# Gated mix of a linear-attention and a softmax-attention block: feature sums on TensorE, denominators in sets of four tiles, projections in four column tiles, placement constants changed

## The chip, the cores and the metric

The kernel runs on one core of one Trainium2 chip. The metric is the device time of one execution in microseconds (us). Before the change it is 698.01 us, the median of three runs (697.92 to 698.1). A measurement of this kernel can tell about 0.2% from no change.

## The reference

Input x has 2048 rows of 512. Two blocks with their own weights read it, each with 32 heads of 16, and a sigmoid gate mixes their outputs row by row.

```python
g = sigmoid((x * gate_w).sum(-1, keepdims=True))
# A, linear attention
q, k, v = heads(x @ A_wqkv)
pq = einsum("bhsd,hdf->bhsf", q, w_phi);  pk = the same of k
phi_q = concat([softmax(pq), softmax(-pq)]);  phi_k = the same of pk
kv = einsum("bhsf,bhsd->bhfd", phi_k, v);  z = phi_k.sum over s
a = merge((phi_q @ kv) / (phi_q @ z + 1e-6)) @ A_wo
# B, softmax attention
b = merge(softmax(q k^T / 4) v) @ B_wo
return g * a + (1 - g) * b
```

Each softmax of A goes over 16 features; its sum is called a feature sum below. There are 64 of them for a row of x: 8 groups of heads (g), plus and minus (s), 4 heads (j). With the exponentials left undivided, the query side needs only the ratio of the plus sum to the minus sum, and the plus sum times 1e-6 in the denominator.

## The kernel before, in words

Softmax attention is most of the work: 2048 score tiles of 128 keys by 512 queries, 64 for each of 32 blocks. A block (b) is one chunk of 512 queries and four heads, which lie in four row strips of 32 on TensorE. A score tile takes one of two ways:

- ScalarE: a pair of tiles goes into two PSUM banks (`add_qk`, L874, product at L870) and one ACTIVATE of 128x1024 makes exponentials (`add_exp`, L961). The two pairs of banks alternate, and the results go to a ring of twelve buffers (E). These pairs, 683 of them, are the slots j = 0 to 682.
- VectorE: the table DN (L31) says how many tiles of each block go there, 682 in all. A tile goes into one of three spare banks (named MISC in the code); VectorE turns it into the bits of an approximate exponential (L947, or two tiles at once, L937); GpSimd adds constants to groups of up to four such tiles (`shifted`, L923), so that three terms with shifted errors are summed.

The products with the values (L982) write psO: four heads lie side by side in four column strips of 32, so that four matmuls make one round. At a block's end VectorE copies psO (L1076), and a chain of small DMAs and VectorE steps divides by the sums.

Everything else runs in the gaps, through the same three spare banks: projections of x and the output projections (`proj`, L664, matmul at L665, full 128x128 weights), the features of the linear branch (`phi`, L1228) and their sums (L1245, one reduce of 1024 elements for each tile of 128 rows), kv and z (`kv_half`, L1275), and on the query side `q_rest` (L1326): for each of 16 row tiles two fills with numerators and denominators together, then for each fill a sum (L1338), a reciprocal (L1341) and a scaling (L1347). `fill` (L635) puts matmuls into a bank, `drain` (L657) is what empties it.

The order on each engine is fixed when the program is built. `Plan.layout` (L178) walks through time with a duration, a priority and dependencies for each operation, picks the next one of each engine, and hands out the banks. Score pairs have the first priority (-100), products with the values -50, further terms T_PRIO, and the rest runs by due times made of constants at L31 to L74 (K_AT and K_PACE for the key side, Q_AT and Q_PACE for the query side, O_AT for outputs, SHIFT for the VectorE tiles of each block). Where TensorE would have nothing to do, and a measure of its recent activity is under ACTIVE[0], the plan puts in a round of four matmuls with zeros (L972). `PE_CLASS` (L45) names three shapes of operation on TensorE: row strips, column strips, and the rest; a change of shape is given 0.105 us in the plan. On the chip each engine then runs its list in order and waits on semaphores.

Of the kernel before, what the change touches and what calls it, by code (L numbers as in the profile page):

```python
# [9 lines left out]
F32 = mybir.dt.float32  # L10
# [20 lines left out]
DN = (6, 20, 18, 20, 26, 22, 22, 20, 22, 18, 20, 18, 22, 20, 22, 22, 26, 22, 22, 28, 22, 24, 22, 26, 18, 22, 26, 18, 20, 20, 28, 20)  # L31
# [4 lines left out]
STICK = 13.196  # L36
UNITS = 564.8
W_AT = 24.588
D_FIRST = 26
# [7 lines left out]
DQ_PRIO, DQ_K = 0.569, 1.599  # L47
KG_AT, KG_PACE, QG_AT, QG_PACE = 21.949, 5.386, 233.655, 11.179
R1_AT, R1_PACE, R2_AT, R2_PACE, R3_AT, R3_PACE = 34.139, 13.567, 134.03, 16.806, 277.767, 5.95
TR_LAT, TR_ISSUE = 3.0, 0.4  # L50
OP_AT, OP_PACE = 603.737, 4.0
SPLIT = (14, 15)
O_AT, O_PACE = 500.39, 18.839
# [3 lines left out]
QK_TOL = (0.374, 0.198)  # L57
TURN_PAD = -0.09
# [3 lines left out]
SHIFT = (-13.58, 13.8, -12.95, 1.31, -8.83, -3.06, 3.59, -1.48, -3.29, 1.96, -3.19, 0.72, 14.4, 6.88, 13.75, 4.89, 8.7, 7.61, 0.14, -2.86, -5.22, -8.15, -0.83, -3.77, 7.8, 2.53, -1.02, -12.66, -5.29, -0.23, -14.57, -12.4)  # L62
P64, W64 = 0.19, 0.21
M_LATE = -26.949
QK_PAD = 0.02
D1_PAIR = 1.13
PAIR_WAIT = 0.05
D_AHEAD = 21.848
CONT = -56.63
# [50 lines left out]
class Plan:  # L120
# [57 lines left out]
    def layout(self):  # L178
# [21 lines left out]
        while left:  # L200
# [30 lines left out]
            for e in ENGINES:  # L231
# [11 lines left out]
                if e == "pe" and last_pe not in (None, "zero") and busy[e] > t - 1e-6:  # L243
# [233 lines left out]
def _build(ctx, nc, A_x, A_wqkv, A_w_phi, A_wo, B_wqkv, B_wo, gate_w, out):  # L477
# [32 lines left out]
    statq = sb([128, 8, 64], F32, name="statq")  # L510
# [16 lines left out]
    denr = sb([128, 2, 32], F32, name="denr")  # L527
# [106 lines left out]

    def fill(prio, mms, reads, banks=None, name="", chunk=1, dur=MM, after=(), cols=NQ, cont=CONT):  # L635

        f = Fill(MISC if banks is None else banks)
        prev = None
        for i in range(0, len(mms), chunk):
# [9 lines left out]
            op.full, op.fill = cols / 2400.0 * len(part), True  # L649
# [14 lines left out]
    def proj(lhs, rhs):  # L664
        return [lambda e, ap, i=i: e.matmul(ap, lhsT=lhs[i], rhs=rhs[i], start=(i == 0), stop=(i == len(lhs) - 1))  # L665
                for i in range(len(lhs))]
# [26 lines left out]
    def k_fill(r, c, prio, banks=None, eng="dve"):  # L693
        f, mm = fill(prio, proj([W_B[:, t, D + 128 * r:D + 128 * (r + 1)] for t in range(KT)],
                                [xT[:, t, NQ * c:NQ * (c + 1)] for t in range(KT)]), ["wbk" if r else "wbk0"] + xk(c), banks,
                     name=f"K{r}.{c}")
# [71 lines left out]
    def q_fill(m, prio, banks=None, after=()):  # L768
# [3 lines left out]
                     name=f"Q{r}.{qc}", after=after)  # L772
# [367 lines left out]
    def last_mm(tile):  # L1140
        return [lambda e, ap: e.matmul(ap, lhsT=oT[:, 3, tile // 4, 128 * (tile % 4):128 * (tile % 4) + 128],
                                       rhs=WoB[:, 3, :], start=True, stop=True)]

    def out_tile(qc, i):
        tile = 4 * qc + i
        if tile in SPLIT:
            f, mm = fill(O_AT + O_PACE * tile, last_mm(tile), [("oT", qc, 3), "WoB"], name=f"O{tile}")
# [5 lines left out]
        f, mm = fill(O_AT + O_PACE * (4 * qc + i), mms, reads, name=f"O{tile}")  # L1153
# [8 lines left out]
    def out_part(n):  # L1162
        tile = SPLIT[n]
        mms, reads = out_mms(tile, range(3), True)
        f, mm = fill(OP_AT + OP_PACE * n, mms, reads, name=f"OP{tile}")
# [5 lines left out]
    def out_last(i):  # L1171
        tile = 12 + i
        mms, reads = out_mms(tile, range(KT), True)
        if i < 2:
            f, mm = fill(-45, mms[:7], reads[:-2] + reads[-1:], banks=MISC + bS[:lowS], name=f"O{tile}", after=last_d1 + o_mms, cont=-45)
            last = P.add("pe", 0.25, -200 + i, lambda e: mms[7](e, f.ap()), reads=[("oT", 3, 3)], after=[mm],
                         name=f"O{tile}.7")
            last.full = 0.215
# [3 lines left out]
        else:  # L1182
            f, mm = fill(-200 + i - 1.5, last_mm(tile), [("oT", 3, 3), "WoB"], banks=bS[:lowS], name=f"O{tile}")
# [30 lines left out]
    def va_fill(st, prio, after):  # L1214
        m, b = st % 8, st % 2
        f, mm = fill(prio, proj([xT[:, t, 128 * st:128 * (st + 1)] for t in range(KT)],
                                [WvA[:, t, :] for t in range(KT)]), ["WvA"] + xk(st // 4), name=f"VA{st}", after=after)
        va_ops.append(mm)
        by = stat[:, b, :].rearrange("p (g s j) -> p g s j", s=2, j=4)
        for s in range(2):  # L1220
# [3 lines left out]
                reads=[("rs", b), ("ss", b)], writes=[("vA", m, s)], name=f"VAe{st}.{s}", last=s == 1)  # L1224
        P.add("pool", 0.3, prio, lambda e: e.tensor_copy(vA[:, m, :, :, 64:68], by), reads=[("rs", b), ("ss", b)],
              writes=[("vA", m, 2)], name=f"VAr{st}")

    def phi(qk, st, prio):  # L1228
# [4 lines left out]
                     xk(st // 4) + [("Wp", qk, t) for t in range(KT)], name=f"P{qk}.{st}",  # L1233
# [3 lines left out]
        def both(e, ap):  # L1237
            for sgn in range(2):
# [4 lines left out]
        e3 = dst.rearrange("p (g f) -> p g f", f=DH)  # L1243
        sums, skey = (stat[:, b, :], ("ss", b)) if qk else (statq[:, st % 8, :], ("sq", st % 8))
        P.add("dve", 1.22, prio, lambda e: e.tensor_reduce(sums, e3, AX.X, ALU.add), reads=[dkey], writes=[skey],  # L1245
              name=f"ss{qk}.{st}")
        if b == 0:
            return
        if qk == 0:
            both_q = statq[:, st % 8 - 1:st % 8 + 1, :].rearrange("p b (g s j) -> p (b g) s j", s=2, j=4)  # L1250
            r3 = ratio[:].rearrange("p b (g j) -> p (b g) j", j=4)
            P.add("dve", 0.4, prio, lambda e: e.reciprocal(r3, both_q[:, :, 1, :]), reads=[("sq", st % 8 - 1), ("sq", st % 8)],
                  writes=["ratio"], name=f"rs{qk}.{st}")
            P.add("dve", 0.25, prio, lambda e: e.tensor_tensor(r3, r3, both_q[:, :, 0, :], ALU.mult),
                  reads=["ratio", ("sq", st % 8 - 1), ("sq", st % 8)], writes=["ratio"], name=f"rt{qk}.{st}").lock = True
            for i in (st - 1, st):
                scaled_q(i, prio)
            return
        P.add("dve", 0.62, prio, lambda e: e.reciprocal(stat[:], stat[:]), reads=[("ss", 0), ("ss", 1)],
              writes=[("rs", 0), ("rs", 1)], name=f"rs{qk}.{st}")  # L1260
        for i in (st - 1, st):
            va_fill(i, prio, [P.ops[-2]] if i == st - 1 else ())
# [148 lines left out]
    for n in range(4):  # L1411
# [3 lines left out]
        for i in range(4 * n, 4 * n + 4):  # L1415
            q_rest(i, Q_AT - 1.0 + Q_PACE * (i + 4))
# [84 lines left out]
```

## Time and profile before

| | |
|---|---|
| median of the runs shown | 698.01 us |
| profiled execution, its own time | 699.61 us |
| its span, first to last instruction | 697.6 us |
| TensorE busy (PE) | 676.3 us, 97% |
| ScalarE busy (ACT) | 671.3 us, 96% |
| VectorE busy (DVE) | 606.4 us, 87% |
| GpSimd busy (POOL) | 369.8 us, 53% |
| exponentials, L961 | 683, 641.6 us |
| feature sums, L1245 | 32, 38.5 us |
| granted TensorE clock | 1.0 throughout |

In the rows of the profile a group of instructions is given by line, engine, operation, output and inputs, shape and count, then its busy time in us and the mean of one in ns, then how long the engine stood idle just before them and what released it. Busy times count overlapping instructions once, so a mean times its count can be more than the busy time. In the timeline the columns are start and length in us, then the group; a line can hold several merged instructions (x3). A line's shape 128*32 is a matmul with 128 rows and 32 columns of weights, 32*128 one with 32 rows and 128 columns. A busy TensorE is not TensorE at its peak, since matmuls are pipelined.

### The profile page before, as it was taken

To read this page: it belongs to the slowest core of one execution; us is meant where nothing else is said; L and a number is where in the kernel's file an instruction comes from. 1 tells how busy PE (TensorE), PEld (TensorE's weight loads), DVE (VectorE), ACT (ScalarE), POOL (GpSimd) and SP (SyncE) were. 2 spreads that over 40 slices of the span, in tenths; PEclk is the share of its full clock that TensorE was granted. 3 is DMA by queue.
4 is the path that set the end of the run, shared out by engine and by line. 5 is a ranking of instruction groups with operands and counts; after the bars stand their busy time and mean duration, and the time that the engine had idled before them with its cause. 6 is when DMAs were issued, how large, how long until landed. Compare 5 with 4: busy or idle time off the path is not lost.

```text
span 697.6 us, 17633 instructions
## 1 busy us (share of the span) xinstructions
PE 676.3 (97%) x7281; PEld 217.7 (31%) x7335; DVE 606.4 (87%) x1020; ACT 671.3 (96%) x754; POOL 369.8 (53%) x407
## 2 busy tenths in 40 slices
PE   9999999999999999999999999999999999999999
PEld 4332233323323223333322322332223322232323
DVE  4689679998988798999987999999999998988882
ACT  6999999999999999999999999999999999999995
POOL 7165246474556552453555674657657555455542
PEclk9999999999999999999999999999999999999999
DMA  6700001001000100100003012223311123314221
GB/s 130 173 12 17 20 18 24 10 11 24 9 18 11 25 10 5 22 10 11 19 11 97 26 27 80 52 49 58 86 51 38 50 46 87 86 48 115 64 58 50
DMA packets 67455, 30.74 MB, mean 44 GB/s; under 512 B 52696, under 2 KB 62296, under 8 KB 67376
## 3 DMA queue, kind: packets, MB, share of 16 engines
q1 hardware_dynamic: 66368, 28.95, 17.7%
q8 instruction: 57, 0.93, 0.6%
q10 hardware_dynamic: 576, 0.52, 0.2%
q0 software_dynamic: 432, 0.15, 0.1%
q14 instruction: 22, 0.18, 0.1%
HBM read 7.87 MB, written 8.88 MB: 24 GB/s over the span
## 4 chain that ended last, share of the span: by engine, by line
PE 63%; DVE 18%; ACT 16%; issue 2%; DMA 1%; SPq 0%; DVEq 0%
PE psO L982 23%; PE psS L870 22%; ACT E_t L961 15%; PE psS L665 11%; PE psO L972 4%; DVE Tx_t L947 3%; DVE Ty_t L947 3%; DVE Wp_t L947 2%; DVE vA_t L947 1%; DVE oT_t L947 1%; ACT phiK_t L1239 1%; DVE stat_t L1245 1%; DVE Tz_t L947 1%; PE psS L735 1%; DMA ld<-Tf_t 1%
## 5 line engine op out<-in xcount | busy, mean ns | idle before, releaser
L961 ACT ACTIVATE E_t<-psS 128x1024 bf16<-128x1024 f32 x683 | 641.6, 1059 | 12.2 <-PE psS L870 5.8
L870 PE MATMUL psS<-qz_t,kTB_t 32*128 32x512 bf16 x2048 | 279.8, 385 | 13.8 <-ACT E_t L961 5.0
L947 DVE TENSOR_SCALAR Tx_t<-psS 128x512 int16<-128x512 f32 x218 | 144.3, 682 | 15.8 <-PE psS L870 15.0
L870 PEld LDWEIGHTS psS<-qz_t,kTB_t 32*128 32x128 bf16 x2048 | 73.4, 91 | 248.4 <-ACT E_t L961 194.1
L982 PE MATMUL psO<-E_t,vaug_t 128*32 128x512 bf16 (+1 forms) x1366 | 112.8, 385 | 0.3 <-issue 0.3
L923 POOL INT64_ADD vA_t<-vA_t x67 | 66.2, 993 | 33.8 <-PE psO L982 23.9
L947 DVE TENSOR_SCALAR Ty_t<-psS 128x512 int16<-128x512 f32 x112 | 74.0, 680 | 7.3 <-PE psS L870 7.0
L923 POOL INT64_ADD Ty_t<-Tx_t x27 | 27.2, 1006 | 64.1 <-DVE Tx_t L947 55.5
L972 PE MATMUL psO<-xT_t,zero_t 128*32 128x512 bf16 x648 | 57.4, 386 | 0.8 <-DVE Tf_t L1076 0.5
L923 POOL INT64_ADD Ty_t<-Ty_t x38 | 38.2, 1004 | 15.8 <-PE psO L982 12.7
L982 PE MATMUL psO<-vA_t,vaug_t 128*32 128x512 bf16 (+1 forms) x480 | 46.1, 383 | 0.0
L947 DVE TENSOR_SCALAR WAT_t<-psS 128x512 int16<-128x512 f32 x58 | 38.2, 679 | 3.6 <-PE psS L870 3.4
L982 PE MATMUL psO<-Ty_t,vaug_t 128*32 128x512 bf16 x398 | 40.5, 384 | 0.0
L947 DVE TENSOR_SCALAR oT_t<-psS 128x512 int16<-128x512 f32 x56 | 37.3, 684 | 3.6 <-PE psS L870 3.6
L947 DVE TENSOR_SCALAR Wp_t<-psS 128x512 int16<-128x512 f32 x58 | 38.9, 682 | 1.2 <-PE psS L870 1.1
L947 DVE TENSOR_SCALAR Tz_t<-psS 128x512 int16<-128x512 f32 x54 | 36.1, 682 | 3.5 <-PE psS L870 3.3
L947 DVE TENSOR_SCALAR vA_t<-psS 128x512 int16<-128x512 f32 x56 | 36.8, 681 | 1.0 <-PE psS L870 0.6
L982 PEld LDWEIGHTS psO<-E_t,vaug_t 128*32 128x32 bf16 x1366 | 24.3, 95 | 41.9 <-issue 39.1
L665 PE MATMUL psS<-Wp_t,xT_t 128*128 128x512 bf16 x116 | 35.6, 384 | 0.9 <-issue 0.5
L665 PE MATMUL psS<-xT_t,WB_t 128*128 128x512 bf16 x96 | 29.7, 385 | 0.8 <-issue 0.6
L923 POOL INT64_ADD vA_t<-Tx_t x20 | 18.2, 910 | 20.6 <-DVE Tx_t L947 17.3
L923 POOL INT64_ADD WoB_t<-oT_t x17 | 16.8, 987 | 21.6 <-DVE oT_t L947 21.3
(160 smaller groups left out, 870.8 us busy)
## 6 DMA issues: line engine op xcount, KB each, us to landing
dpq<-EA_t SPq DMA_DIRECT2D x16, 256.0 KB, 2.1
Rb_t<-lr SPq DMA_DIRECT2D x120, 32.0 KB, 1.8
dpo<-kv_t SPq DMA_DIRECT2D x16, 128.0 KB, 1.8
qz_t<-qz_t SPq DMA_DIRECT2D x120, 16.0 KB, 1.8
Tf_t<-Tf_t SPq DMA_DIRECT2D x60, 32.0 KB, 2.0
WB_t<-in_B_wqkv_dram SPq DMA_DIRECT2D x3, 384.0 KB, 4.4
out_dram<-WvA_t SPq DMA_DIRECT2D x8, 128.0 KB, 1.9
out_dram<-WB_t SPq DMA_DIRECT2D x6, 128.0 KB, 1.8
```

The lines of the kernel that those rows point to most:

```text
L665: return [lambda e, ap, i=i: e.matmul(ap, lhsT=lhs[i], rhs=rhs[i], start=(i == 0), stop=(i == len(lhs) - 1)) for i in range(len(lhs))]
L735: mms = [lambda e, ap, i=i, t=t: e.matmul(ap[:, 256 * i:256 * (i + 1)], lhsT=xT[:, t, NQ * c + 128 * (2 * hf + i):NQ * c + 128 * (2 * hf + ...
L870: return e.matmul(bank, lhsT=kT_B[32 * i:32 * i + 32, ROW[b // 2] % 2, 128 * kt:128 * (kt + 1)], rhs=qz[32 * i:32 * i + 32, b // 2 % 4, b ...
L923: op = P.add("pool", P64 + W64 * size, d_prio(g["ts"][0]) - 5.0 + (0.0 if key == "s" else M_LATE), lambda e: e.int64_add(words(dst), words ...
L947: ops.append(drain(f, mm, "dve", 0.70, d_prio(d), lambda e, ap, q=q: e.tensor_scalar(quarter(tb, q).bitcast(I16), ap, EXPB, 0.0, op0=ALU.a ...
L961: op = P.add("act", 0.051 + 0.4267 * n, 0.0, lambda e: e.activation(Ebuf[:, j // 2 % EPAIRS, 512 * SZ[0] * (j % 2):512 * SZ[0] * (j % 2) + ...
L972: ins = e.matmul((psO if bank is None else bank)[32 * i:32 * i + 32, :], lhsT=zero[:], rhs=xT[:, 0, 0:NQ], start=bank is not None, stop=ba ...
L982: return e.matmul(psO[32 * i:32 * i + w, :], lhsT=vaug[:, kt, o:o + w], rhs=rhs, start=start, stop=stop, tile_position=(0, 32 * i), skip_g ...
L1239: ins = e.activation(dst.rearrange("p (g s c) -> p s g c", s=2, c=64)[:, sgn, :, :], ap.rearrange("p (g c) -> p g c", c=64), ACTF.Exp, sca ...
L1245: P.add("dve", 1.22, prio, lambda e: e.tensor_reduce(sums, e3, AX.X, ALU.add), reads=[dkey], writes=[skey], name=f"ss{qk}.{st}")
```

## The change

1. The feature sums move from VectorE to TensorE. For two row tiles together, 16 matmuls with an identity as weights add up the 16 features of each head in PSUM; matmul n reads every 16th element, from n on, of both tiles, 128 columns. VectorE then takes reciprocals straight from PSUM (and, on the query side, copies the plus sums).
2. The denominators of the linear branch are made for four row tiles at once (`z_rest`: 32 matmuls of 4 columns, one sum, one reciprocal), and the numerators of a row tile in one fill of eight matmuls with one scaling of 128x512.
3. Each projection matmul (128x128 weights, 512 columns) becomes four matmuls of 32 weight columns in the four column strips, and has the shape of the products with the values in the plan (`"col"`, class 1).
4. The constants of the plan are other ones, among them DN (sum 682 before, 686 after).

```diff
-DN = (6, 20, 18, 20, 26, 22, 22, 20, 22, 18, 20, 18, 22, 20, 22, 22, 26, 22, 22, 28, 22, 24, 22, 26, 18, 22, 26, 18, 20, 20, 28, 20)
+DN = (6, 20, 18, 20, 26, 26, 22, 20, 22, 18, 20, 18, 16, 18, 22, 22, 26, 22, 20, 28, 20, 24, 22, 26, 18, 22, 26, 18, 22, 24, 28, 26)
...
-STICK = 13.196
+STICK = -4.158
...
-ACTIVE = (1.3, 0.464, 0.202, 0.534)
-PE_CLASS = {"qk": 0, "dq": 0, "pv": 1, "term": 1, "zero": 1}
-T_PRIO = 24.777
+ACTIVE = (1.766, 0.586, 0.369, 0.433)
+PE_CLASS = {"qk": 0, "dq": 0, "pv": 1, "term": 1, "zero": 1, "col": 1}
+T_PRIO = 63.423
...
-OP_AT, OP_PACE = 603.737, 4.0
+OP_AT, OP_PACE = 662.103, 4.0
...
-O_AT, O_PACE = 500.39, 18.839
+O_AT, O_PACE = 464.624, 20.512
...
-G_DEEP = 9
-K_AT, K_PACE, Q_AT, Q_PACE = 75.929, 11.329, 287.016, 9.116
+G_DEEP = 13
+K_AT, K_PACE, Q_AT, Q_PACE = 75.929, 11.329, 323.294, 8.77
...
+    def columns(e, out, lhsT, rhs, start, stop):
+        for i in range(4):
+            ins = e.matmul(out[32 * i:32 * i + 32, :], lhsT=lhsT[:, 32 * i:32 * i + 32], rhs=rhs, start=start, stop=stop,
+                           tile_position=(0, 32 * i))
+        return ins
...
     def proj(lhs, rhs):
-        return [lambda e, ap, i=i: e.matmul(ap, lhsT=lhs[i], rhs=rhs[i], start=(i == 0), stop=(i == len(lhs) - 1))
+        return [lambda e, ap, i=i: columns(e, ap, lhs[i], rhs[i], i == 0, i == len(lhs) - 1)
                 for i in range(len(lhs))]
...
-        e3 = dst.rearrange("p (g f) -> p g f", f=DH)
-        sums, skey = (stat[:, b, :], ("ss", b)) if qk else (statq[:, st % 8, :], ("sq", st % 8))
-        P.add("dve", 1.22, prio, lambda e: e.tensor_reduce(sums, e3, AX.X, ALU.add), reads=[dkey], writes=[skey],
-              name=f"ss{qk}.{st}")
         if b == 0:
             return
+        m = st % 8 - 1 if qk else 0
+        pair = (phiK if qk else EA)[:, m:m + 2, :].rearrange("p b (g f) -> p b g f", f=DH)
+        mms = [lambda e, ap, n=n: e.matmul(ap[:, 0:128].rearrange("p (b g) -> p b g", b=2), lhsT=ident[:], rhs=pair[:, :, :, n],
+                                           start=(n == 0), stop=(n == DH - 1)) for n in range(DH)]
+        f, mm = fill(prio, mms, ["ident"] + [("phiK" if qk else "EA", m), ("phiK" if qk else "EA", m + 1)], name=f"S{qk}.{st}",
+                     chunk=4, dur=0.057, cols=128)
...
-        P.add("dve", 0.62, prio, lambda e: e.reciprocal(stat[:], stat[:]), reads=[("ss", 0), ("ss", 1)],
-              writes=[("rs", 0), ("rs", 1)], name=f"rs{qk}.{st}")
+        drain(f, mm, "dve", 0.9, prio, lambda e, ap: e.reciprocal(flat(stat[:]), ap[:, 0:128]), writes=[("rs", 0), ("rs", 1)],
+              name=f"rs{qk}.{st}")
...
+    def z_rest(n, prio):
+        mms = [lambda e, ap, j=j, g=g: e.matmul(ap[:, 32 * j + 4 * g:32 * j + 4 * g + 4], lhsT=qT(g)[:, 128 * j:128 * (j + 1)],
+                                                rhs=kzbd[:, g, 64:68], start=True, stop=True) for j in range(4) for g in range(8)]
+        f, mm = fill(prio, mms, [("phiQT", g) for g in range(8)] + ["kz1"], name=f"Z{n}", chunk=8, dur=0.028, cols=60, after=n_ops[-1:])
+        n_ops.append(mm)
+        dr = denr[:, n % 2, :]
+        plus = flat(statq[:, 4 * (n % 2):4 * (n % 2) + 4, :])
+        drain(f, mm, "dve", 0.25, -3, lambda e, ap: e.scalar_tensor_tensor(dr, plus, 1e-6, ap[:, 0:128], ALU.mult, ALU.add),
+              reads=[("sq", 4 * (n % 2) + j) for j in range(4)], writes=[("dr", n % 2)], name=f"na{n}")
+        P.add("dve", 0.9, -3, lambda e: e.reciprocal(dr, dr), reads=[("dr", n % 2)], writes=[("dr", n % 2)], name=f"nb{n}")
```

The lines left out pass the name "col" to the fills of projections, shape the numerators into one fill, and give other values to the remaining constants (SHIFT for all blocks, the due times of the value and key projections, and pads of a few hundredths).

More of the change, by code (lines that the diff above doesn't have):

```diff
@@ L242, in layout @@
                     active = sum(w * (y - max(x, t - WINDOW)) for x, y, w in streams) / WINDOW
-                if e == "pe" and last_pe not in (None, "zero") and busy[e] > t - 1e-6:
+                if e == "pe" and last_pe not in (None, "zero", "col") and busy[e] > t - 1e-6:
                     want = {"qk": "dq", "dq": "dq"}.get(last_pe, "term")
@@ L648, in fill @@
                        after=after if prev is None else [prev], name=f"{name}.{i}")
-            op.full, op.fill = cols / 2400.0 * len(part), True
+            op.full, op.fill, op.kind = cols / 2400.0 * len(part), True, kind
             if prev is None:
@@ L1182, in out_last @@
         else:
-            f, mm = fill(-200 + i - 1.5, last_mm(tile), [("oT", 3, 3), "WoB"], banks=bS[:lowS], name=f"O{tile}")
+            f, mm = fill(-200 + i - 1.5, last_mm(tile), [("oT", 3, 3), "WoB"], banks=bS[:lowS], name=f"O{tile}", kind="col")
             with_part(tile, f, mm)
@@ L1216, in va_fill @@
         f, mm = fill(prio, proj([xT[:, t, 128 * st:128 * (st + 1)] for t in range(KT)],
-                                [WvA[:, t, :] for t in range(KT)]), ["WvA"] + xk(st // 4), name=f"VA{st}", after=after)
+                                [WvA[:, t, :] for t in range(KT)]), ["WvA"] + xk(st // 4), name=f"VA{st}", after=after, kind="col")
         va_ops.append(mm)
```

102 lines of the change are left out of this document (46 added, 56 removed).

## The prediction

> **What bounds the kernel now.** I read the page's first part, then the groups by shape, the chain that ended last, and the timeline of ScalarE, of the stretch from 300 to 312 us and of the end.
>
> ```profile
> PE 676.3 (97%) x7281; PEld 217.7 (31%) x7335; DVE 606.4 (87%) x1020; ACT 671.3 (96%) x754; POOL 369.8 (53%) x407
> ...
> L961 ACT ACTIVATE E_t<-psS 128x1024 bf16<-128x1024 f32 x683 | 641.6, 1059 | 12.2 <-PE psS L870 5.8
> ```
>
> TensorE and ScalarE are both nearly full, but TensorE's 97% holds filler: the rows of L972, products with zeros put where the plan had nothing else, are 57.4 + 5.0 us. It needs 676.3 - 62.4 = 614 us. ScalarE has no filler. What an exponential costs when nothing holds it up is read from unbroken runs in the chain:
>
> ```profile
> 48.77 12.04 ACT E_t L961 x13
> ...
> 168.04 0.99 ACT phiK_t L1239 x2
> ...
> 327.26 17.53 ACT E_t L961 x19
> ```
>
> 12.04 / 13 = 0.926 and 17.53 / 19 = 0.923 us for each; 0.98 us for the two activations of a feature tile (0.99 with the step to the next). So 683 x 0.923 + 32 x 0.98 = 661.8 us of work from 8.7 (start of the first exponential) to 687.6 (end of the last, below). 678.9 us passed, so ScalarE stood or was slowed for 17.1 us. The five longest pauses:
>
> ```profile
> 137.94 2.86 ACT L961 ACTIVATE E_t<-psS 128x1024 bf16<-128x1024 f32 x3 [0.96 <-PE psS L870]
> ...
> 346.25 17.93 ACT L961 ACTIVATE E_t<-psS 128x1024 bf16<-128x1024 f32 x19 [1.47 <-PE psO L982]
> ...
> 376.61 10.33 ACT L961 ACTIVATE E_t<-psS 128x1024 bf16<-128x1024 f32 x11 [1.15 <-PE psS L870]
> 388.15 1.94 ACT L961 ACTIVATE E_t<-psS 128x1024 bf16<-128x1024 f32 x2 [1.21 <-PE psO L982]
> ...
> 450.15 4.89 ACT L961 ACTIVATE E_t<-psS 128x1024 bf16<-128x1024 f32 x5 [1.14 <-PE psO L982]
> ```
>
> They sum to 5.9 us. TensorE is named, but it runs a fixed order and is itself held: ahead of 137.9 a score tile waited 0.21 us for a VectorE eviction, ahead of 376.6 one waited 1.03 us for the paired eviction of L937, which stood behind two reciprocals. Ahead of 388 and 450 TensorE ran filler (four rounds, three rounds) before the last products of a block, which need VectorE's tiles and GpSimd's additions. VectorE was busy 18.8 to 19.9 us of every 20 between 380 and 440. Ahead of 346.3 stands the one 1.45 us mask multiply of L1299. The other 11 us are delays of a few tenths, where a slot holds more TensorE work than 0.92 us.
>
> TensorE's prices, from 300 to 312 us:
>
> ```profile
> 306.98 0.40 PE L982 MATMUL psO<-Ty_t,vaug_t 128*32 128x512 bf16 x4
> ...
> 307.20 0.39 PE L982 MATMUL psO<-oT_t,vaug_t 128*32 128x512 bf16 x4
> 307.53 0.45 PE L870 MATMUL psS<-qz_t,kTB_t 32*128 32x512 bf16 x4
> ```
>
> A round of four 32-column products follows the one before after 0.22 us; the step to score tiles (32*128, rows) takes 0.33. A change of shape costs 0.1 us, into and out of full 128*128 products too (0.32).
>
> And the end:
>
> ```profile
> 679.14 8.44 ACT L961 ACTIVATE E_t<-psS 128x1024 bf16<-128x1024 f32 x9
> ...
> 686.03 0.39 PE L870 MATMUL psS<-qz_t,kTB_t 32*128 32x512 bf16 x2
> ...
> 694.33 2.99 PE L972 MATMUL psS<-xT_t,zero_t 128*32 128x512 bf16 x52
> 694.44 0.69 ACT L1179 ACTIVATE WB_t<-psS,gT_t 128x512 bf16<-128x512 f32 x1 [1.47 <-PE psS L665]
> ```
>
> After the last scores at 686.03 TensorE works without a gap for 8.3 us, until filler starts at 694.33; the last output tile is scaled at 694.44, and its store ends the span 3.2 us later. The end hangs on TensorE, not on ScalarE, which was done at 687.6.
>
> **The change, part by part.** Counts come from the order in which each kernel's instructions stand.
>
> *Exponentials.* Sum of DN 682 -> 686: 1362 score tiles are left to ScalarE, 681 pairs. 2 x 0.923 = **-1.8 us**, on the path.
>
> *VectorE.*
>
> ```profile
> L1245 DVE TENSOR_REDUCE stat_t<-phiK_t 128x64 f32<-128x1024 bf16 x16 | 19.3, 1208 | 3.8 <-ACT phiK_t L1239 3.8
> L1245 DVE TENSOR_REDUCE statq_t<-EA_t 128x64 f32<-128x1024 bf16 x16 | 19.2, 1208 | 3.2 <-ACT EA_t L1239 3.2
> ...
> L722 PE MATMUL psS<-WB_t,xT_t 128*128 128x128 bf16 x128 | 10.6, 221 | 0.2 <-DVE Ty_t L947 0.2
> ...
> L1341 DVE RECIPROCAL denr_t<-denr_t 128x16 f32<-128x16 f32 x32 | 7.2, 239 | 0.3
> ```
>
> Gone: both reduce rows, 38.5; 32 reciprocals, 7.2; 32 sums of L1338, 4.9; 32 scalings of L1347 (128x256), 14.8: 65.4 us. New: 16 scalings of 128x512 from PSUM at 0.745 (the same operation at L1136: 0.746), 11.9; 4 reciprocals of 128x128 at 0.946 (L1259), 3.8; 4 sums of 128x128, between 0.16 (L1338, 16 elements) and 0.48 (256), say 0.3, 1.2; 8 copies of 64, between 0.155 (L1194) and 0.43 (L1292), say 0.2, 1.6. The 16 other reciprocals stay and read PSUM; I know no row for that and add nothing. Evictions of score tiles: 612 -> 606 single at 0.682, 35 -> 40 paired at 1.22: +2.0. Net 65.4 - 20.5 = 45 us less: VectorE 606 -> 561 us (80%). None of this is on the path by itself; it counts by what waits for VectorE.
>
> *TensorE.* Feature sums: 256 products with 128 moving columns. Bounds: 0.056 us each, the spacing of L722 in bursts (contiguous operand), and 0.106, that of the transposes L1356. I take 0.056, the row with the same kind of instruction: +14.3 us (up to 27.1). Denominators by themselves: 128 products of 4 columns at 0.025 (spacing at L1190, one column), +3.2; the numerators stay 128. Two more rounds for the four tiles, +0.4; two score pairs fewer, -0.4. Projections: 440 products become 440 rounds of four, 0.22 either way. Filler: 724 -> 584 products, 35 rounds, -7.7. Changes of shape 1481 -> 1411: -7.0. Sum +2.8 us in the order; without filler +10.5, so it needs 625 us where ScalarE needs 660. What hides the sums is filler and waits for ScalarE; where a stretch has neither, its 0.9 us per pair of tiles delays the next scores. In the trace, TensorE's work between score pairs is over 0.92 us in 245 slots by these prices, in the changed order in 252: I expect the small delays (11 us) to stay as they are.
>
> [...] The sums take every 16th bf16 element, one for each 32 bytes. [...]
>
> *Waits that are added.* The sums wait for both tiles' exponentials and hold one of three spare PSUM banks over some four slots; behind them on TensorE stands everything, score pairs too. The same tiles' reduce waited for the exponentials before (3.8 and 3.2 us idle), without a bank. 16 such fills and 4 for denominators come, 16 numerator fills go. SP's and POOL's instructions are the same but for two additions on POOL (53% busy).
>
> *Pauses.* VectorE with 45 us less, and later with room, should take away the pauses that it and its tiles cause: 0.96, 1.15, 1.21, 1.14, and 0.31 us at 127.8 where two feature tiles meet: **-4.8 us**. The one at 346.3 stays, as the mask multiply does. Bounds: 0 (the order of TensorE is as long, and TensorE is what is late next) and -10 (half the small delays go too).
>
> *The end.* After the last scores the old order has 36 rounds (4 of probabilities, 32 of output projections) in 8.3 us. The new one has 56: one output tile and the rest of another, three sets of probabilities and six more rounds of VectorE's terms stand behind the last scores. 56 x 0.22 + 0.1 = 12.4: **+4.1 us**. It cannot go earlier, since the order is fixed. The last block's chain on VectorE (transpose 0.70, reciprocal 0.25, multiply 0.42, transpose 0.71) ends about 9.3 us after the last scores (30 rounds, then 2.7 as in the trace); its first user stands behind 44 rounds, at 9.8: hidden, by little.
>
> **Sum.** -1.8 - 4.8 + 4.1 = -2.5. The profiled execution took 699.6 (span 697.6 and 2.0 around it) and would be 697.1; it stands 1.6 above the median of 698.0, so the median becomes **695.5 us**.
>
> **Rivals.**
> *A, more goes than the pauses.* Fewer changes of shape (-7.0) fall into slots over 0.92 us, and half of the 11 us of small delays go: 698.0 - 1.8 - 10.3 + 4.1 = 690. For: a projection beside probabilities or terms now costs no change of shape. Against: 252 slots are still over 0.92.
> *B, slower: the work behind the last scores decides.* The pauses stay or are replaced by waits for banks and sums, and the longer end is paid: 698.0 - 1.8 + 4.1 = 700.3. It is slower by over 0.2% from the point where less than 0.9 us of pauses goes. For: TensorE's order is 2.8 us longer, and in it the pauses' nearest cause is TensorE. Against: VectorE's share in four of five.
> *C, slow sums.* At 0.106 a product, 12.8 us more; TensorE's waits for ScalarE take some: 695.5 + 10 = 705.5. L722 speaks for 0.056. [...]
> *D, the change doesn't do what it says.* If four column products ran one after another, 440 x 3 x 0.22 = 290 us more. The rows of L982, four starts within one 0.22 us round, exclude it nearly.
>
> **Chances.** Forecast 0.37 (694 to 699), A 0.23, B 0.27 (699 to 702.5), C 0.08, D 0.01; 0.04 for other waits, slower. 0.2% is 1.4 us, about what a measurement tells from no change. Faster (below 696.6): 0.25 of the forecast and A, 0.48. Same: 0.12 of the forecast and 0.04 of B, 0.16. Slower 0.36. The range takes in A, the forecast and B and leaves C out: 689.5 to 703; the forecast alone, 694 to 699.
>
> **What would show it.** 681 exponentials at an unbroken 0.92; L1245 gone and VectorE at 561 us; sums spaced 0.056 (C: 0.1); a step of 0.22 between rounds of projections and of probabilities; last scores near 679.4 in a span of 695; 12.4 us from them to the last projection. Last scores at 684 would be B. It is wrong if ScalarE's lost time (17.1) grows, or a wait for a PSUM bank shows ahead of score tiles.

## The result and the profile after

The kernel after takes 779.67 us (median of four runs, 779.49 to 781.12) where the kernel before takes 697.96: a ratio of 1.1175 (95% interval 1.1156 to 1.1194). It is 12% slower. The profiled execution took 781.12 us, with a span of 779.0 us and a mean granted TensorE clock of 0.93; before, the clock was 1.0.

The page of the kernel after, first its totals, then the granted clock in 40 slices of the span (9 is 90% or more of full speed), then three groups by shape:

```profile
PE 770.3 (99%) x8907; PEld 247.2 (32%) x8907; DVE 575.6 (74%) x923; ACT 676.6 (87%) x752; POOL 372.0 (48%) x409
...
PEclk9999979899999998877999989899897989998999
...
L967 ACT ACTIVATE E_t<-psS 128x1024 bf16<-128x1024 f32 x681 | 646.3, 1055 | 83.7 <-PE psS L876 79.0
...
L1252 PE MATMUL psS<-EA_t,ident_t 128*128 128x128 bf16 x128 | 32.9, 408 | 0.4 <-ACT EA_t L1244 0.4
L1252 PE MATMUL psS<-phiK_t,ident_t 128*128 128x128 bf16 x128 | 31.9, 410 | 0.0
```

The counts are those of the forecast: 681 exponentials, L1245 gone. ScalarE has two exponentials fewer than before (its busy time is 676.6 us, 671.3 before) and VectorE is busy 31 us less. ScalarE's share is down to 87%, since it stood 83.7 us ahead of its exponentials, 79.0 of them for score tiles. TensorE is busy 99% and is what is late. Two rows stick out: the sum products (L1252) are busy 64.8 us together, where 14.3 was forecast, and one of them lasts 0.41 us. The clock has holes all along the span.

One burst shows both. The timeline of the kernel after from 96 to 116 us (start, length, group):

```profile
100.24 2.94 PE L1252 MATMUL psS<-phiK_t,ident_t 128*128 128x128 bf16 x12
...
103.43 1.09 PE L1252 MATMUL psS<-phiK_t,ident_t 128*128 128x128 bf16 x4
103.54 1.02 ACT L967 ACTIVATE E_t<-psS 128x1024 bf16<-128x1024 f32 x1 [2.02 <-PE psS L876]
...
106.94 0.61 PE L876 MATMUL psS<-qz_t,kTB_t 32*128 32x512 bf16 x2
...
112.42 0.65 PE L988 MATMUL psO<-WoA_t,vaug_t 128*32 128x512 bf16 x4
...
112.84 0.65 PE L988 MATMUL psO<-oT_t,vaug_t 128*32 128x512 bf16 x4
...
114.28 0.38 PE L988 MATMUL psO<-Tx_t,vaug_t 128*32 128x512 bf16 x4
...
114.50 0.38 PE L988 MATMUL psO<-Ty_t,vaug_t 128*32 128x512 bf16 x4
...
115.25 1.02 ACT L967 ACTIVATE E_t<-psS 128x1024 bf16<-128x1024 f32 x1 [2.09 <-PE psS L876]
```

Twelve sum products last 2.94 us and one 0.41: (2.94 - 0.41) / 11 = 0.23 us from one to the next, four times the 0.056 of the forecast. The next scores come late and ScalarE stands 2.02 us. That would be one delay per burst. But up to ten us later the rounds of L988, 0.22 us apart before, follow each other after 0.42 (112.42 to 112.84) and a pair of score products lasts 0.61 us, not 0.39; from 114.28 on they have their old 0.22 and 0.38. The stretches of the same trace, with the granted clock in the third column from the end (TensorE, weight loads, VectorE, ScalarE, GpSimd, clock, DMA share, GB/s):

```profile
96.00:100.00 4.00, 4.00 (x58) 1.12 (x50) 1.65 (x4) 4.00 (x6) 1.86 (x2) 1.00 0.03 8
100.00:103.80 3.80, 3.80 (x24) 1.61 (x17) 0.69 (x1) 1.78 (x3) 0.00 (x0) 0.99 0.08 19
104.50:113.50 9.00, 9.00 (x67) 1.91 (x70) 3.79 (x6) 6.13 (x8) 0.73 (x3) 0.50 0.08 12
114.50:118.00 3.50, 3.50 (x49) 1.53 (x41) 2.45 (x4) 2.75 (x3) 2.76 (x3) 1.00 0.16 47
```

TensorE is busy in every one of these stretches, and yet its clock is 0.50 for ten us behind the burst. The trace has 15 such stretches, 109.2 us in all, 3.4, 6.8, 10.2 or 13.7 us long, and each begins 2.2 to 5.4 us after the first product of a burst, with 10 to 14 sum products in the 4.5 us ahead of it. Of the 16 bursts one, at 467.3 us, is followed by no such stretch.

So the first theory: **the stride**. A sum product reads every 16th element, which makes it four times as long, and while TensorE waits for its columns the clock is taken down. Its rivals: **the order** (the new list of work and the waits for banks are bad whatever a product costs), **VectorE or the banks** (a wait of another kind), and, for the clock, that it falls for a cause of its own.

### The profile page after: what moved, and what is told of

Its sections match the earlier page's. It is cut to its first block, busy times and chain, and to the rows that moved or that the text cites. A ratio compares the mean times of both kernels' runs of the same rounds, so it can differ in the third digit from the quotient of the medians.

```text
span 779.0 us, 20738 instructions
## 1 busy us (share of the span) xinstructions
PE 770.3 (99%) x8907; PEld 247.2 (32%) x8907; DVE 575.6 (74%) x923; ACT 676.6 (87%) x752; POOL 372.0 (48%) x409
## 4 chain that ended last, share of the span: by engine, by line
PE 80%; ACT 17%; DVE 2%; issue 0%
PE psO L988 27%; PE psS L876 25%; ACT E_t L967 17%; PE psS L637 13%; PE psS L1252 8%; PE psO L978 4%; PE psS L741 1%; PE psS L1349 1%; PE psS L1337 1%; PE psS L978 0%; PE psS L589 0%; DVE Tx_t L953 0%; DVE oT_t L953 0%; ACT phiK_t L1244 0%; DVE qz_t L781 0%; DVE Ty_t L953 0%
## 5 line engine op out<-in xcount | busy, mean ns | idle before, releaser
L967 ACT ACTIVATE E_t<-psS 128x1024 bf16<-128x1024 f32 x681 | 646.3, 1055 | 83.7 <-PE psS L876 79.0
L876 PE MATMUL psS<-qz_t,kTB_t 32*128 32x512 bf16 x2048 | 287.6, 403 | 4.5 <-ACT E_t L967 3.2
L988 PE MATMUL psO<-E_t,vaug_t 128*32 128x512 bf16 x1362 | 120.6, 409 | 0.0
L953 DVE TENSOR_SCALAR Ty_t<-psS 128x512 int16<-128x512 f32 x110 | 73.3, 683 | 12.7 <-PE psS L876 12.4
L929 POOL INT64_ADD vA_t<-vA_t x67 | 66.5, 1000 | 24.2 <-PE psO L988 13.1
L953 DVE TENSOR_SCALAR oT_t<-psS 128x512 int16<-128x512 f32 x62 | 40.9, 683 | 9.4 <-PE psS L876 9.3
L988 PE MATMUL psO<-vA_t,vaug_t 128*32 128x512 bf16 x480 | 46.7, 393 | 0.0
L978 PE MATMUL psO<-xT_t,zero_t 128*32 128x512 bf16 x500 | 46.4, 401 | 0.2 <-DVE Tf_t L1082 0.2
L988 PE MATMUL psO<-Ty_t,vaug_t 128*32 128x512 bf16 x412 | 43.2, 400 | 0.0
L953 DVE TENSOR_SCALAR vA_t<-psS 128x512 int16<-128x512 f32 x50 | 33.4, 684 | 12.6 <-PE psS L876 12.4
L637 PE MATMUL psS<-Wp_t,xT_t 128*32 128x512 bf16 x512 | 42.4, 391 | 0.0
L988 PEld LDWEIGHTS psO<-E_t,vaug_t 128*32 128x32 bf16 x1362 | 26.5, 97 | 42.8 <-issue 37.0
L637 PE MATMUL psS<-xT_t,WB_t 128*32 128x512 bf16 x464 | 39.1, 402 | 1.0 <-DVE stat_t L1269 1.0
L1252 PE MATMUL psS<-EA_t,ident_t 128*128 128x128 bf16 x128 | 32.9, 408 | 0.4 <-ACT EA_t L1244 0.4
L1252 PE MATMUL psS<-phiK_t,ident_t 128*128 128x128 bf16 x128 | 31.9, 410 | 0.0
```

The costliest lines, as they stand in the source:

```text
L637: ins = e.matmul(out[32 * i:32 * i + 32, :], lhsT=lhsT[:, 32 * i:32 * i + 32], rhs=rhs, start=start, stop=stop, tile_position=(0, 32 * i))
L876: return e.matmul(bank, lhsT=kT_B[32 * i:32 * i + 32, ROW[b // 2] % 2, 128 * kt:128 * (kt + 1)], rhs=qz[32 * i:32 * i + 32, b // 2 % 4, b ...
L929: op = P.add("pool", P64 + W64 * size, d_prio(g["ts"][0]) - 5.0 + (0.0 if key == "s" else M_LATE), lambda e: e.int64_add(words(dst), words ...
L953: ops.append(drain(f, mm, "dve", 0.70, d_prio(d), lambda e, ap, q=q: e.tensor_scalar(quarter(tb, q).bitcast(I16), ap, EXPB, 0.0, op0=ALU.a ...
L967: op = P.add("act", 0.051 + 0.4267 * n, 0.0, lambda e: e.activation(Ebuf[:, j // 2 % EPAIRS, 512 * SZ[0] * (j % 2):512 * SZ[0] * (j % 2) + ...
L978: ins = e.matmul((psO if bank is None else bank)[32 * i:32 * i + 32, :], lhsT=zero[:], rhs=xT[:, 0, 0:NQ], start=bank is not None, stop=ba ...
```

## The experiments

Times are medians; ratios are to the kernel before, run on the same chip.

**1. The same order, other addresses.** One line is changed: a sum product reads 64 neighbours of each tile (e1), or 512 neighbours in all (e2).

```diff
-        pair = (phiK if qk else EA)[:, m:m + 2, :].rearrange("p b (g f) -> p b g f", f=DH)
+        pair = (phiK if qk else EA)[:, m:m + 2, :]
...
-                                           rhs=pair[:, :, :, n],
+                                           rhs=pair[:, :, 64 * n:64 * n + 64],
```

> The changed kernel with the order of every engine the same, but each of the 256 sum products reads 64 + 64 neighbouring elements in place of every 16th (it adds up other elements, so the sums are not the feature sums). Theory 1, the distance between the elements read makes the products slow (0.232 us in place of 0.056) and the slow products bring TensorE's clock down: spacing 0.056 us, clock 1.0 throughout, 45 us of products gone and the stretches at half clock too, 695 to 702 us. Rival 2, the order and the placement let the clock fall (fewer filler rounds, projections in column strips): stretches at half clock stay, over 740 us. Rival 3, the products are slow because of the identity weights or because all 16 add into the same 128 columns of a bank: spacing stays 0.23, 775 to 785 us.

> The changed kernel with the same order, each sum product reading 512 neighbouring elements (other sums, 512 columns of a bank written): it should take 0.216 us by the spacing of 512-column products, nearly the 0.232 of the strided ones, but the array gets a column in every cycle. It parts the time of the products from the clock. Theory 1a, the clock falls because the strided products feed the array a column only now and then: clock 1.0 throughout, 256 x 0.16 = 41 us over the kernel of e1 less what waits for ScalarE take up, 730 to 742 us. Rival, the clock falls because score pairs come late and TensorE waits: stretches at half clock stay, 765 us or more.

e1 takes 700.58 us (1.0024, 1.0008 to 1.004). Its page, the totals and the clock:

```profile
PE 689.1 (99%) x8907; PEld 233.6 (33%) x8907; DVE 571.5 (82%) x923; ACT 670.2 (96%) x752; POOL 372.5 (53%) x409
...
PEclk9999999999999999999999999999998999999999
```

And its sum products among the groups by shape:

```profile
L1252 PE MATMUL psS<-EA_t,ident_t 128*128 128x128 bf16 x128 | 10.6, 221 | 0.4 <-ACT EA_t L1244 0.4
L1252 PE MATMUL psS<-phiK_t,ident_t 128*128 128x128 bf16 x128 | 9.6, 220 | 0.0
```

The list of work is the same instruction by instruction, and 79 us are gone with the addresses alone: the order and the banks can't be the cause. The products are 0.056 us apart, and the clock has one hole of 6.8 us, at 523.6. The sum products nearest to it ended 5.8 us before; right ahead of it stand 24 of the new denominator products, of 4 columns each, and two waits of TensorE (0.51 and 0.21 us).

e2 takes 738.47 us (1.0587, 1.0562 to 1.0611), with clock 1.000 throughout in its trace. Its products are as long as the strided ones (0.216 us apart), but a column arrives every 0.42 ns (0.216 us for 512), where the strided ones bring one every 1.8 ns (0.232 us for 128):

```profile
PE 726.5 (99%) x8907; PEld 240.9 (33%) x8907; DVE 572.6 (78%) x923; ACT 672.5 (91%) x752; POOL 372.5 (51%) x409
...
L1252 PE MATMUL psS<-EA_t,ident_t 128*128 128x512 bf16 x128 | 31.1, 381 | 0.4 <-ACT EA_t L1244 0.4
L1252 PE MATMUL psS<-phiK_t,ident_t 128*128 128x512 bf16 x128 | 30.1, 380 | 0.0
```

The two parts of the loss come apart here. Longer products: 738.5 - 700.6 = 38 us (of 256 x 0.16 = 41 us of TensorE, so nearly all of it is on the path). The rest, 779.7 - 738.5 = 41 us: 256 x 0.016 = 4 us of it are the still longer products, and some 37, what is left, the clock.

**2. What sets a product's price.** The step between the columns (e3), then runs of neighbours at a fixed distance (e13); both sums of something else.

```diff
+        step = (16, 8, 4, 2, 1, 12, 6, 3)[st // 2]
...
+                                           rhs=pair[:, :, slice(n, n + 63 * step + 1, step)],
```

> The changed kernel with the same order and another step between the elements that the sum products read for each pair of row tiles (16, 8, 4, 2, 1, 12, 6, 3 elements of 2 bytes, once on the key side and once on the query side; other sums). [...] Rival, the time grows with the bytes spanned: step 2 twice, step 4 four times 0.056, and no more from 8 on. [...] Time between e1 and the changed kernel, 715 to 765 us.

> The kernel after, whose sum products read something else than the features that they should sum (so its sums are others): in turn runs of 1, 2, 4 and 8 neighbouring values, each run at a distance that spreads 128 columns over 1024 bytes for each of the two tiles; on the key side the runs begin on a multiple of 16 bytes, on the query side 14 bytes behind one, so that a run of 2 or more lies across two pieces of 16 bytes. By the pieces fetched (0.0018 us each): key side 0.228, 0.114, 0.057, 0.056 us for runs of 1, 2, 4, 8; query side 0.228 for 1 and 2, 0.114 for 4, 0.057 for 8. By the bytes spanned alone (1024 in all cases): 0.228 us in all eight. By the step inside a run alone (neighbours are free): 0.056 us for runs of 2 and more on both sides. Time 720 to 750 us, since about half of the products are slow.

Each was run once, e3 in 731.75 us and e13 in 735.62, both as expected. From product to product, in us (median of a burst at full clock; "pieces" are the 16-byte pieces of memory that 128 columns touch):

| step, elements | 1 | 2 | 3 | 4 | 6 | 8 | 12 | 16 |
|---|---|---|---|---|---|---|---|---|
| pieces | 16 | 32 | 48 | 64 | 96 | 128 | 128 | 128 |
| measured | 0.056 | 0.062 | 0.090 | 0.118 | 0.173 | 0.228 | 0.226 | 0.232 |

| neighbours in a run | 1 | 2 | 4 | 8 |
|---|---|---|---|---|
| key side, runs within a piece | 0.228 | 0.118 | 0.056 | 0.056 |
| query side, runs across two pieces | 0.228 | 0.228 | 0.112 | 0.070 |

The price is 0.0018 us for each piece, within 0.004 us of all values but one, and never under 0.056. It is flat from 16 bytes on, so the distance itself costs nothing, and the same two neighbours cost 0.118 or 0.228 us as they lie within a piece or across two. The one that is off is the last (0.070 where 0.057 was expected). Two columns in a piece are not enough for the 0.056 us of neighbours (step 4 has two, and takes 0.118 us); four nearly are (step 2, 0.062).

**3. What takes the clock down.** If it falls because too few columns arrive, more work for TensorE must bring it back. In the kernel after, one idle product of 384 neighbouring columns into an unused part of the bank follows every second sum product (e9) or each of them but the last (e10).

```diff
+            if n % 2 == 0 and n < DH - 1:
+                e.matmul(ap[:, 128:512], lhsT=ident[:], rhs=base[:, n % 2, 0:384], start=False, stop=False, skip_group_check=True)
```

> The changed kernel with the same order and, behind every second sum product, one more product with the identity over 384 neighbouring elements into the unused columns of the same bank (its result is not used): 120 to 128 products of 0.16 us, about 20 us of work more on TensorE. Theory 1a, the half clock follows from an array that gets a column only now and then: during the sums the share of cycles with a column rises from about 0.24 to 0.44, the half-clock stretches go or get few, and more work takes less time: 755 to 770 us. Rival, the half clock follows from late score pairs, or from the length of the burst: stretches stay, 795 us or more.

> The same with one such product behind every sum product but the last: 240 products of 0.16 us, 38 us of work more, share of cycles with a column about 0.55. Theory 1a: clock 1.0 nearly throughout and about the time of e2 plus 35 to 42, 772 to 782 us. Rival: half-clock stretches stay, 810 us or more.

e9 takes 764.49 us (1.0943, 1.0924 to 1.0963): 128 products more than the kernel after, and 15 us less. The stretches of e9 (columns as above), then the burst:

```profile
100.00:104.00 4.00, 4.00 (x24) 1.98 (x20) 0.69 (x1) 1.34 (x2) 0.00 (x0) 1.00 0.10 22
104.00:108.00 4.00, 4.00 (x38) 1.29 (x36) 2.29 (x4) 2.64 (x3) 0.41 (x2) 1.00 0.08 15
```

```profile
100.46 0.62 PE L1255 MATMUL psS<-phiK_t,ident_t 128*128 128x128 bf16 x2
100.90 0.34 PE L1258 MATMUL psS<-phiK_t,ident_t 128*128 128x384 bf16 x1
101.08 0.62 PE L1255 MATMUL psS<-phiK_t,ident_t 128*128 128x128 bf16 x2
```

Two sum products and one idle one take 0.62 us (100.46 to 101.08) and hold 640 columns; at 0.216 us for 512, as in e2, that is 0.27 us of columns, 44% of the time, where the sums alone have 0.054 / 0.23 = 23%. At 44% the clock stayed, at 23% it fell: behind the 16 bursts of e9 there is no stretch but one of 6.8 us (mean clock 0.996), at the place in the order where e1 has its hole, among the denominator products. An idle product adds 0.627 - 2 x 0.232 = 0.163 us, all 128 of them 21 us. If all of that lands on the path, the clock had cost about 15 + 21 = 36 us: the second measure of it, beside the 37 of e2. e10 has the same clock and 240 idle products (39 us), and takes 782.84 us (1.1218), 3 more than the kernel after: 39 - 3 = 36 again, and just over the 772 to 782 that were expected.

The traces bear this out without the sums as well. The changes of the clock in a trace lie on a grid of 3.41 us. For each window of that grid one can add up the columns of the matmuls that start in it (0.422 ns for each, by the 0.216 us for 512; a matmul on a quarter of the array counts as a quarter). In the kernel after, the 15 windows ahead of a fall hold columns for 0.22 to 0.40 of the time, and 174 of the other 179 at full clock for more than 0.40. Over the fifteen traces here that have a fall, 37 of the 45 windows at full clock with 0.30 or less are followed by one, 36 of the 105 between 0.30 and 0.40, and 1 of some 2930 above. The falls in the kernels without slow products (e1, e5, e7, e8, e11, e12, e14, e16) are among them. What decides between 0.30 and 0.40 stays open.

In the trace of the kernel after the clock is 1.0 or 0.5, and the stretches at 0.5 last 3.4 us or a multiple of it. It did not fall for an idle TensorE: in the 3.4 us ahead of a fall TensorE is busy in the profile all the time for 12 of the 15 falls, and for 85 to 89% of it for the other three.

**4. Parts alone, and other constants.** e4, e7 and e8 put one part into the kernel before (feature sums; four column tiles; denominators), e5 takes the feature sums out of the kernel after, e6 tells the plan the measured price of a sum product.

```diff
-                     chunk=4, dur=0.057, cols=128)
+                     chunk=4, dur=0.232, cols=557, kind="sum")
```

> The kernel before with the first part of the change alone: the 32 reduces become sum products with every 16th element (given 0.057 us each in the plan, as in the change) and 16 copies of 128x128 out of PSUM; constants, projections and denominators as before. Theory 1 (slow strided products, then half clock): spacing 0.232, stretches at half clock, 760 to 790 us. Rival, the other parts or the constants are needed for the loss: under 735 us.

> The changed kernel with the feature sums back on VectorE (32 reduces of 1.21 us), denominators in sets of four, column strips and all constants as changed; the plan lays the order out anew. Theory 1: clock 1.0, no slow products, 694 to 704 us. Rival 2, the constants or the column strips are what costs: over 720 us.

> The changed kernel with the same computation, but the plan gives a sum product its measured 0.232 us and counts it as a quarter of the array's activity, so that it can place score pairs and rounds of zeros around it. Theory 1: the products still take 256 x 0.232 = 59 us of TensorE, which has no room for 45 us more; the half-clock stretches should shrink: 730 to 755 us. If the loss came from the plan's wrong price alone: under 715 us. If the clock can't be kept by a plan: 770 us or more.

> The kernel before with the third part alone: projections in four column strips, counted by the plan as the shape of the value products; all constants as before. By the prediction's terms about 70 changes of shape fewer, 7 us of TensorE's order: 690 to 698 us. If the constants, made for another order, fit no longer: 700 to 720 us. If four column products were slower than one full product: a step over 0.23 us between rounds.

> The kernel before with the second part alone: denominators for four row tiles at once, numerators in one fill; constants as before. VectorE has 10 us less. By the prediction 694 to 698 us; if the constants fit no longer, 700 to 715 us; clock 1.0 in both.

| | us | ratio, 95% | clock of the profiled run |
|---|---|---|---|
| e4, before + feature sums | 814.17 | 1.1665 (1.1628 to 1.1701) | 0.939 |
| e5, after without them | 719.13 | 1.0309 (1.0288 to 1.033) | 0.991 |
| e6, after, plan with 0.232 | 783.06 | 1.1233 (1.1186 to 1.1281) | 0.946 |
| e7, before + column tiles | 719.1 | 1.0307 (1.0287 to 1.0326) | 0.993 |
| e8, before + denominators | 707.63 | 1.0147 (1.013 to 1.0164) | 0.995 |

The sums are the loss in both directions: 116 us more with them in the kernel before (e4 has 99 us of half clock in 14 stretches), 61 us less without them in the kernel after, and both are more than a new order alone was seen to cost (35 and 42 us, below). None of the five times lies where the first expectation put it: e4 is above 790 us, e5 above 704, e6 above 755 (and over the 770 that stood for a clock that no plan can keep), e7 and e8 above 698, where they were expected if the constants fit no longer. That e5, e7 and e8 are slower than before by 10 to 21 us can't be put down to the parts: each of these edits gives the plan other durations, and the whole order comes out another way, with constants chosen for another list. How much that alone costs was measured in the kernel before, with one constant changed by 1 (K_AT, then T_PRIO):

> The kernel before with one constant of the plan moved: K_AT 76.929 in place of 75.929, so that the key side of the linear branch is due 1 us later; the same work, laid out anew. If an order laid out anew costs 10 us and more whatever the change (the losses of e5, e7 and e8): 705 to 720 us, with score pairs later here and there. If those losses came from the parts themselves: 697 to 700 us.

> The kernel before with another constant moved a little: T_PRIO 25.777 in place of 24.777 (priority of the further terms); the same work. As for e11: 705 to 720 us if a new order costs by itself, 697 to 700 us if not.

733.25 us (1.0505, 1.0484 to 1.0526) and 739.68 (1.0597, 1.0576 to 1.0618): 35 and 42 us for an edit that changes no operation, far more than expected. So the parts can only be judged in the order of the kernel after, and e4 to e8 leave them open. e6 falls under the same: with the price known to the plan the clock still fell (85 us at half clock, 16 stretches), and whether the order or the price of waiting ate the rest is open.

**5. The change with neighbours.** The features are laid out as (head group, feature, head), so that a product reads 32 runs of four heads, 8 bytes each, and forms the sums that it should; the order is kept (e14). The projection weights get their new column order where VectorE evicts them, eight times. e15 evicts in the order of the writes; e16 makes the new order once, on POOL, in the small block matrix instead.

```diff
+        pair = (phiK if qk else EA)[:, m:m + 2, :].rearrange("p b (h f j) -> p (b h) f j", f=DH, j=4)
...
+            Wp[:, t, D * qk:D * (qk + 1)].rearrange("p (g f j) -> p g j f", f=DH, j=4), ap.rearrange("p (g j f) -> p g j f", j=4, f=DH)),
```

> The same sums are computed as in the kernel after, in the same order of work on every engine, but the features lie in memory as (head group, feature, head), so that the four heads' values of one feature are neighbours: a sum product reads 32 runs of 4 neighbouring values (8 bytes), 128 bytes apart, and fetches 32 places in place of 128. If the price of a product is set by the 16-byte pieces that it fetches (0.0018 us each, from the 0.232 us of 128), 32 of them are hidden behind the 0.056 us of 128 columns: the products are spaced 0.056 us, the clock stays at 0.99 or above, and the time is that of the kernel with neighbours read, 697 to 702 us. If any step between the columns costs as much as the distance that it spans, the products stay near 0.2 us and the time near 780 us. If the layout only costs elsewhere (the eight evictions that write the projection weights 32 bytes apart, the scaling of the minus half with its ratio taken over again for every feature), the products are at 0.056 us and VectorE has more than its 571.5 us.

> The same as the kernel with the features laid out as (head group, feature, head), but the eight evictions go through their elements in the order in which they are written (neighbours written, PSUM read 64 bytes apart) and not in the order in which they are read. If only writes 8 bytes apart are slow, the evictions take 0.68 us and the time is 697 to 702 us; if the side that is strided does not matter, they stay at 1.30 us and the time at 704 us.

> The same as the kernel with the features laid out as (head group, feature, head), but the new order is made once, by one more copy on POOL of the small block matrix from which the projection weights are made, so that the eight evictions of those weights are written in a row again, as in the kernel after; the order of all else stays. If the 4 us that the last scores came later than with neighbours read (685.3 against 681.8 us) came from those evictions (1.30 us in place of 0.68, eight times, 5.0 us of VectorE ahead of 63 us, and the half-clock stretch at 43.4 us behind them), the evictions are back at 0.68 us, VectorE is at 571 us, and the time is 697 to 702 us. If it came from anything else in the layout (the scaling of the minus half, the sums read in runs of 8 bytes), the time stays at 703 to 705 us. That the copy on POOL comes too late for the products that read it, at 35.8 us, would show as a wait of PE there and cost up to 1 us.

e14 takes 704.26 us (1.0082, 1.0068 to 1.0097), with its products 0.056 us apart. VectorE pays elsewhere; the eviction of the projection weights in e14, then in e15:

```profile
L1217 DVE CAST Wp_t<-psS 128x512 bf16<-128x512 f32 x8 | 10.0, 1303 | 0.0
```

```profile
L1217 DVE CAST Wp_t<-psS 128x512 bf16<-128x512 f32 x8 | 5.3, 679 | 0.0
```

Written 8 bytes apart, an eviction takes 1.30 us; read 64 bytes apart and written in a row, 0.68. With that, e15 takes 699.62 us (1.0023, 1.0013 to 1.0033) and e16 700.19 (1.0028, 1.0015 to 1.004): the price of the layout was those writes. With the clock left out the step is much the same: the one run of e14 at a mean clock of 1.000 took 702.73 us. No kernel here beats the one before. Three runs of e15 had a mean clock of 1.000 and took 698.61 to 698.88 us; the others had 0.995 or 0.998, which stands for one or two times 3.4 us at half clock, and took 699.5 to 701.1.

## Why the prediction was wrong

Forecast 695.5 us in a range of 689.5 to 703, faster; measured 779.67, outside. By its steps:

*TensorE, the step that failed.* "Bounds: 0.056 us each ... and 0.106 ... I take 0.056": it is 0.232 us. That is 256 x 0.176 = 45 us more of TensorE, and filler and waits for ScalarE, which were to hide the sums, don't: of the 41 us more of TensorE that e2 has than e1, 38 land on the path. Both bounds came from rows that read neighbours or whole tiles, so neither held for the operand at hand, and the upper one was no bound.

*Rival C* had the mechanism, slow sums, with 0.08, and priced it from the 0.106 row: 705.5 us. The two rows of before that it names, 0.056 and 0.106, show no product that is slow by its addresses; e3 shows one, with 0.056 us for neighbours and 0.232 for a step of 16.

*The clock, which no step had.* A term for a fall of the clock is missing altogether: some 36 to 37 us (e2, e9, e10). The clock is 1.0 throughout in the trace of before, and I took it as given. The change brings products that keep TensorE busy with few columns, and the plan, which places zeros by its own measure of activity, had them down as 128 columns in 0.057 us.

*The rest* can be held against e15, which has the order of the kernel after and products at 0.056 us. Its profiled execution took 698.79 us with clock 1.000. Its page, its one pause of ScalarE over 0.6 us, and its end:

```profile
PE 687.6 (99%) x8907; PEld 234.1 (34%) x8907; DVE 571.4 (82%) x923; ACT 669.9 (96%) x752; POOL 372.1 (53%) x409
```

```profile
591.34 5.79 ACT L970 ACTIVATE E_t<-psS 128x1024 bf16<-128x1024 f32 x6 [1.88 <-PE psO L991]
```

```profile
680.06 0.39 PE L879 MATMUL psS<-qz_t,kTB_t 32*128 32x512 bf16 x2
```

```profile
692.26 0.38 PE L640 MATMUL psS<-WoB_t,oT_t 128*32 128x512 bf16 x2
...
692.71 0.69 ACT L1187 ACTIVATE WB_t<-psS,gT_t 128x512 bf16<-128x512 f32 x1 [1.04 <-PE psS L981]
```

- Exponentials, -1.8: as forecast.
- Pauses, -4.8: five with 5.9 us became one with 1.9, and ScalarE's lost time, 17.1 us, is 13.1: -4.0. That it comes near is partly luck: the pause at 346.3, which was to stay, went too (the mask multiply took 0.68 us in e15, 1.45 before), and the one of 1.9 us, at 591.3, is new and was in no step. The small delays stayed, 11.2 us in both, as forecast; rival A, which took half of them, is out.
- Last scores at 680.06 (forecast 679.4, before 686.03).
- The end, +4.1: from there to the end of the last projection 692.64 - 680.06 = 12.6 us (forecast 12.4, before 8.3), +4.3; the last store then took 0.7 us more: +5.0.
- Column rounds 0.22 us apart: as forecast; rival D is out.
- VectorE 571.4 us, not 561: the instructions that went, 65 us long, had partly lain over their neighbours, and busy time counts that once. With the lengths of all instructions added up, 672.4 us became 625.6, 46.8 less, near the forecast's 45; what lay over a neighbour went from 66 us to 54.

Together -1.0 us between two profiled executions, where -2.5 was forecast. Between ordinary runs it is the other way round: 698.7 at full clock against 697.8, +0.9, and +1.8 between the medians. The profiled execution of before is 1.6 us above the median of its own runs and 1.8 above that of the runs beside e15; the profiled execution of e15 is 0.8 below its median. So the step "it stands 1.6 above the median ..., so the median becomes 695.5" fails too: part of the pauses whose end was counted as a gain may have been in that execution only. Which of them, no other trace of before tells; it stays open. Without the stride the outcome is near rival B (700.3), though the pauses did go.

## What to carry to other kernels

Price an operand by its addresses, not by its shape: for a matmul's moving operand, count the 16-byte pieces that its columns touch (0.0018 us each here), and lay data out so that at least four bf16 columns share one (128 columns took 0.062 us with four, 0.118 with two). A TensorE that the profile shows busy can still be starved (columns for 23% of the time in the bursts of the kernel after), and there the clock was 0.5 for the 3.4 to 13.7 us that followed; look at the granted clock behind the first burst of a new kind of product. And in a kernel whose order comes from tuned constants, compare parts only in one and the same order.

## What the runs showed of the hardware

- 128 bf16 columns took max(0.056, 0.0018 x pieces) us, for pieces of 16 bytes (e3 and e13; 0.070 in place of 0.057 where runs of 8 straddle). In the kernel after the strided products kept their 0.232 us at half clock (18 steps), where the rounds of L988 went from 0.22 to 0.42.
- With columns for 23% of the time the clock fell 2.2 to 5.4 us after a burst began (kernel after, 15 of 16 bursts); with 44% it stayed (e9). By windows of 3.41 us, over fifteen traces: above 0.40 one fall in some 2930 windows, at 0.30 or less 37 in 45.
- 128 added products made the kernel after 15 us faster (e9).
- Half clock costs this kernel about 0.36 us per us (an estimate: 36 to 37 us for some 100 us in the kernel after, whose ordinary runs had a mean clock of 0.936 over 777 us), or 0.3 to 0.5 (e1: 700.6 to 701.2 us at a mean clock of 0.995, 6.8 us of half clock, against 697.7 and 698.5 at 1.0).
- On VectorE it was the written side that counted, for a copy of 128x512 out of PSUM: 1.30 us written 8 bytes apart (e14), 0.68 read 64 bytes apart and written in a row (e15).
